# Four heads' scores in one run of matmuls, two PSUM banks for the rest, a filled fourth tile, and ACT as the issuer of attention's stores

## The chip, the cores and the metric

The kernel runs on one core of a Trainium2 chip. The metric is device time in microseconds (us) of one execution; lower is better. The engines are PE (matrix products; PEld is its loading of weights), DVE, ACT and POOL (elementwise work), and SP, which here only issues DMAs. ACT can issue DMAs too; an engine that issues one is occupied while it does so.

## What is computed

Attention over 4 batches, 12 heads, 448 positions and 64 columns per head, in which the heads are mixed twice, then two feed-forward layers over the 1792 rows of 768 columns that attention leaves:

```python
scores = scale * np.matmul(q, k.transpose(0, 1, 3, 2))
scores = np.einsum('bhij,hg->bgij', scores, w_pre)
scores = scores - np.max(scores, axis=-1, keepdims=True)
attn = np.exp(scores)
attn = attn / (np.sum(attn, axis=-1, keepdims=True) + 1e-09)
attn = np.einsum('bhij,hg->bgij', attn, w_post)
x = np.matmul(attn, v)            # then (B, H, S, D) -> (B*S, H*D)
x = (1 / (1 + np.exp(-(x @ w_gate))) * (x @ w_val)) @ w_out
h = np.maximum(x @ w_in, 0.0)
out = h * h @ w_out2
```

## The kernel before

**Attention.** Each batch's 448 rows are cut into four row tiles of 110, 110, 110 and 118 rows, 16 tiles in all; two tiles make a half batch (a chunk, eight in all). `scores(n, p)` makes the scores of two heads (a pair) for tile `n`: four records of PE in the trace (L171), which ACT copies out of PSUM for the one head and DVE for the other (`e`), and which SP stores into `g` so that ten rows of twelve heads lie on 120 partitions. In the tile of 118 rows the last eight rows need a second, small store for each head (L196).

The 180 groups of ten rows are 180 steps of one loop. A step `s` does, in order: `premix(s)`, the first mixing of heads (three matmuls, L219, into `ps_m`); what is pending from the step before (`flush`: the copy `mixed` of postmix's result by DVE, L273, or the copy `valued` of the values by ACT, L305, with its store to `xs`, L306); `maximum(s)` (DVE, L227); `exponent(s-1)` (ACT, L235); `normal(s-2)`, the sum's reciprocal (DVE, L241 and L244) and the weights `wn` that carry it (POOL, L246); and `split(s+2)`, which splits the scores of two steps later into a high part (ACT, `gh`, L209) and a rest (POOL, `gl`, L210). Then a small planner puts in what is owed: `scores` of the next tile, `postmix` (eight records, L261, three steps or more behind) or, once a half batch is mixed, one `values` for each of six steps (16 records, L290). A step's kinds are written here as s (a pair of scores), p (a postmix) and v (values). The planner has a budget for a step and estimated costs:

```python
MW, PW, VW, SW, STEP = 0.62, 0.82, 1.66, 1.04, 2.41
...
            left_over = STEP - MW
            ready = front and front[0][0] <= s
            if ready and due(s):
                next_scores()
```

**Order of DMAs.** SP takes its DMAs in the order of the program: `q` and `k` tiles, `g` stores, `xs` stores, and the six loads `vraw` of a half batch (two heads each, four buffers, so that the fifth load can go when the first values are done). DMAs of SP and ACT use eight semaphores, DMAHW0 to DMAHW7, one after another in the order of the program whichever engine issues them; a DMA is issued only when the one before it on its semaphore has landed. `order` rows show these waits in brackets.

**PSUM.** Eight banks: two for `ps_m`, two for scores (`ps_q`), four (`ps_b`) for postmix and values, which the first tile's scores share.

**The layers after it.** `mlp` is a generator. The attention loop lets it advance in the last 112 steps (`EARLY`), in steps without a postmix, and more freely once all scores are made (`closed`): it loads weights (`w_raw`), splits them (ACT L480, DVE L486 to L509, POOL `w` L520 and `wl` L534) and splits attention's finished columns (`xr`, `xh`, `xl` L596). Its matmuls (L666) stand between the last half batch's values and then fill the rest.

Of the kernel before, what the change touches and what calls it, by code (L numbers as in the profile page):

```python
# [7 lines left out]
F32 = mybir.dt.float32  # L8
# [5 lines left out]
PSUM = bass.MemoryType.PSUM  # L14
DRAM = bass.MemoryType.DRAM

P = 128
JP = 112
GI = 10
# [1 line left out]
LAG = 3  # L21
LA = 5
NA = 9
MW, PW, VW, SW, STEP = 0.62, 0.82, 1.66, 1.04, 2.41
KB = 10
EARLY = 112
EM = 2
# [9 lines left out]

def blocks(b, i0, i1):

    n = (i1 - i0) // GI  # L40
    return [(0, 4), (4, n)] if b == i0 == 0 else [(0, n)]


def row_order(b, i0, i1):

    rows = []
    for g0, g1 in blocks(b, i0, i1):
        rows += [i0 + g * GI + r for r in range(GI) for g in range(g0, g1)]
    return rows + list(range(i0 + len(rows), i1))


def attention(tc, q, k, v, w_pre, w_post, xs, B, H, S, D):
# [10 lines left out]
    nc = tc.nc  # L63
    JT = S // JP
    NP = H // 2
    SCALE = 1.0 / float(D) ** 0.5

    tiles, groups, chunks = [], [], []
# [7 lines left out]
            chunks[-1][4] = len(groups)  # L76
            tiles.append((b, i0, i1 - i0))
    NG = len(groups)
    IM = max(t[2] for t in tiles)
    GT = -(-IM // GI)  # L80
    CM = max(c[2] - c[1] for c in chunks)
    KM = GI * H

    with ExitStack() as ctx, ExitStack() as mid, ExitStack() as left:
        kw = dict(side="right")
# [4 lines left out]
        pa = mid.enter_context(tc.tile_pool(name="a_a", bufs=NA, **kw))  # L90
        pg = mid.enter_context(tc.tile_pool(name="a_g", bufs=2, **kw))
        ph = mid.enter_context(tc.tile_pool(name="a_h", bufs=3, **kw))
        ps_b = ctx.enter_context(tc.tile_pool(name="ps_b", bufs=4, space=PSUM, **kw))
        ps_q = mid.enter_context(tc.tile_pool(name="ps_q", bufs=2, space=PSUM, side="left"))
        ps_m = mid.enter_context(tc.tile_pool(name="ps_m", bufs=2, space=PSUM, side="left"))
        pk = left.enter_context(tc.tile_pool(name="a_k", bufs=KB, side="left"))
        p2 = left.enter_context(tc.tile_pool(name="a_2", bufs=2, side="left"))
# [42 lines left out]
        k_t, q_t = {}, {}  # L140
# [3 lines left out]
            nc.sync.dma_start(out=k_t[b, p], in_=k[b, p])  # L144

        def q_load(n, p0=0, p1=NP):
            b, i0, isz = tiles[n]
            if p0 == 0:
                q_t[n] = p2.tile([P, NP, IM], F32, tag="q", name="q")
            n0, n1 = (b * S + i0) * H * D, (b * S + i0 + isz) * H * D  # L150
            x = q[n0:n1].rearrange("(d p i) -> d p i", d=P, p=NP)
            nc.sync.dma_start(out=q_t[n][:, p0:p1, :isz], in_=x[:, p0:p1])


        g_t, second = {}, []

        def scores(n, p):

            b, i0, isz = tiles[n]
            if p == 0:  # L160
                g_t[n] = pg.tile([KM, GT, S], F32, tag="g", name="g")
            kt = k_t.pop((b, p)) if i0 + isz == S else k_t[b, p]
            ps = [
                ps_b.tile([P, S], F32, tag="b", name="ps_s")
                if n == 0 and p % 2
                else ps_q.tile([P, S], F32, tag="q", name="ps_s")
                for _ in range(2)
            ]
            for o in range(2):
                r = slice(o * D, (o + 1) * D)  # L170
                nc.tensor.matmul(  # L171
                    ps[o][:isz], lhsT=q_t[n][r, p, :isz], rhs=kt[r], start=True, stop=True
                )
            if n == 0 and p >= 3:
                e = [pa.tile([IM, S], F32, tag="a", name="e0") for _ in range(2)]
            else:
                t = p4.tile([IM, 2, S], F32, tag="e", name="e")
                e = [t[:, o] for o in range(2)]
            to = g_t[n].rearrange("(r h) g j -> h r g j", h=H)
            for o in range(2):  # L180
                if o:
                    nc.vector.tensor_copy(e[o][:isz], ps[o][:isz])
                else:
                    nc.scalar.copy(e[o][:isz], ps[o][:isz])
                e0 = 0
                for m, (g0, g1) in enumerate(blocks(b, i0, i0 + isz)):
                    e1 = e0 + (g1 - g0) * GI
                    move = (to[2 * p + o, :, g0:g1], e[o][e0:e1])
                    if m:
                        second.append(move)  # L190
                    else:
                        queue = nc.scalar if n == 0 and o and p in (1, 3, 4, 5) else nc.sync
                        queue.dma_start(out=move[0], in_=move[1])
                    e0 = e1
                if e0 < isz:
                    nc.sync.dma_start(out=to[2 * p + o, : isz - e0, g1], in_=e[o][e0:isz])  # L196


        a_t = {}
# [3 lines left out]
        def split(s):  # L203
            n, r0, rows = groups[s][:3]
            kk = rows * H
            hi = ph.tile([KM, S], F32R, tag="gh", name="gh")
            lo = ph.tile([KM, S], F32R, tag="gl", name="gl")
            x = g_t[n][:kk, r0 // GI]
            nc.scalar.copy(hi[:kk], x)  # L209
            nc.gpsimd.tensor_tensor(out=lo[:kk], in0=x, in1=hi[:kk].bitcast(F32), op=ALU.subtract)  # L210
            parts[s] = (hi[:kk], lo[:kk])
# [39 lines left out]
        ap, pending = {}, []  # L251
# [49 lines left out]
        def valued(c, h, ps):  # L301
            b, i0, i1 = chunks[c][:3]
            w = i1 - i0
            xo = po.tile([P, CM], F32, tag="xo", name="xo")
            nc.scalar.copy(xo[:, :w], ps[:, :w])  # L305
            nc.sync.dma_start(out=xs[b][h * D : (h + 2) * D, i0:i1], in_=xo[:, :w])  # L306


        NT = len(tiles)
# [5 lines left out]
        def load_next(load, order):  # L315
            x = next(order, None)
            if x is not None:
                load(*x)
# [4 lines left out]
            front += [(max(starts[n - 1] - 2, 0), starts[n] - LA, n, p) for p in range(NP)]  # L323
        def due(s):

            return any(z - 1 - i <= s for i, (_, z, _, _) in enumerate(front[:NP]))

        back = []
        for c, ch in enumerate(chunks):
            back += [(postmix, PW, s) for s in range(ch[3], ch[4])]  # L330
            back += [(values, VW, c, h) for h in range(0, H, 2)]
        bpos, closed, posted, behind = 0, False, {}, 0

        def next_scores():
            _, _, n, h = front.pop(0)
            scores(n, h)
            if tiles[n][1] + tiles[n][2] == S:
                load_next(k_load, k_order)
            if h == NP - 1 and n + 1 < NT:
                q_load(n + 1)  # L340

        def flush():
            now, pending[:] = list(pending), []
# [3 lines left out]
        for p in range(0, NP, 2):  # L347
            q_load(0, p, p + 2)
            load_next(k_load, k_order)
            load_next(k_load, k_order)  # L350
        q_load(1)
        masks()
        for p in range(NP):
            scores(0, p)
        mixers()
        for m, (x, y) in enumerate(second):
            (nc.scalar if m % 3 == 1 else nc.sync).dma_start(out=x, in_=y)  # L357
        for s in range(2):
            split(s)
        for s in range(NG + 30):  # L360
            if s < NG:
                premix(s)
            flush()
            if s < NG:
                maximum(s)
            if s in (4, 5, 6, 7):
                load_next(v_load, v_order)
            if 8 <= s < 8 + KB - NP:
                load_next(k_load, k_order)
            if 1 <= s <= NG:  # L370
                exponent(s - 1)
            if 2 <= s < NG + 2:
                normal(s - 2)
            if s + 2 < NG:
                split(s + 2)
            left_over = STEP - MW
            ready = front and front[0][0] <= s
            if ready and due(s):
                next_scores()
                ready, left_over = False, left_over - SW  # L380
            while bpos < len(back) and (left_over > 0.5 or s >= NG):
                f, cost, *x = back[bpos]
                if f is postmix:
                    if x[0] > s - LAG:
                        break
                    posted[groups[x[0]][3]] = s
                elif posted[x[0]] == s:
                    if s < NG:
                        break
                    flush()  # L390
                elif posted[x[0]] == s - 1 and ready:
                    next_scores()
                    ready = False
                if len(pending) > 3:
                    flush()
                f(*x)
                if f is values and (x[1] + 2) % HV == 0:
                    pending.append((load_next, v_load, v_order))
                bpos += 1
                left_over -= cost  # L400
                if f is postmix and x[0] == NG - 1:
                    flush()
                    mid.close()
                if s >= NG:
                    yield 3 if bpos == len(back) or back[bpos][0] is values else 2
            if ready and left_over > 0.4:
                next_scores()
            if not front and not closed:
                left.close()
                closed = True  # L410
            if NG - EARLY <= s < NG:
                behind += 1
                if closed:
                    yield 2
                elif behind >= 3 and s not in posted.values():
                    behind -= 3
                    yield 1
# [406 lines left out]
```

## Time and profile before

| what | value |
|---|---|
| median of 3 executions | 1508.63 us (1508.27 to 1511.84) |
| the profiled execution | 1510.66 us |
| its span in the trace | 1508.9 us |
| mean granted clock of PE | 0.988 of full speed |
| attention, to the last `ps_v` | 0 to 537.3 us |
| matmuls of the layers alone | 537.3 to 1505.4 us |

The span is what the trace covers; the execution's own time is 1.8 us longer. The profiled execution is 2.0 us above the median. Times in the trace are counted from the start of the span.

### The profile page before, as it was taken

Reading aid. Unit: us, or ns where it says so; the run is one execution under the profiler, and the core shown is the slowest. Engines: PE = TensorE matmul, PEld = TensorE weight load, DVE = VectorE, ACT = ScalarE, POOL = GpSimd, SP = SyncE. Lnnn points to the kernel's source line nnn. Section 1 sums busy time; section 2 is a strip of 40 time slices with the busy share of each in tenths; the row PEclk is TensorE's granted clock in tenths of the full one; section 3 lists DMA queues with packets and bytes.
Section 4 is the critical chain, followed back from the end, with each engine's and each line's share of the span. In section 5 each row is a group of like instructions: output and inputs, shape, how many; then the busy total and the mean of one; then the engine's idle time right before and its main releaser. Section 6 shows DMA issues by size and latency. Waiting matters only on the chain.

```text
span 1508.9 us, 22075 instructions
## 1 busy us (share of the span) xinstructions
PE 1468.7 (97%) x8028; PEld 1245.0 (83%) x8028; DVE 809.2 (54%) x1367; ACT 579.6 (38%) x1192; POOL 708.8 (47%) x583
## 2 busy tenths in 40 slices
PE   6989989999998999999999999999999999999999
PEld 3657657667676889999999999999999999999998
DVE  4648657667678577778889999911111001333000
ACT  4545645655655333333234433312222122333111
POOL 3646656766679355555455555532222221222221
PEclk8989999999999999999999999999999999999999
DMA  5453553545534354444444446631211111112221
GB/s 178 140 163 113 150 156 119 168 132 172 167 116 141 113 170 174 156 166 164 158 157 159 163 166 205 217 96 53 63 43 62 53 53 53 53 53 67 75 72 39
DMA packets 87976, 185.47 MB, mean 123 GB/s; under 512 B 18236, under 2 KB 55100, under 8 KB 87868
## 3 DMA queue, kind: packets, MB, share of 16 engines
q1 hardware_dynamic: 87348, 183.28, 38.4%
q8 instruction: 63, 1.03, 0.3%
q10 hardware_dynamic: 520, 0.79, 0.2%
q14 instruction: 45, 0.37, 0.1%
HBM read 107.75 MB, written 37.75 MB: 96 GB/s over the span
## 4 chain that ended last, share of the span: by engine, by line
PE 95%; DMA 2%; POOL 1%; DVE 1%; issue 1%; SPq 0%; ACT 0%; ACTq 0%; POOLq 0%; DVEq 0%
PE ps L666 66%; PE ps_p L261 9%; PE ps_m L219 8%; PE ps_s L171 6%; PE ps_v L290 5%; DMA vraw<-in_v 1%; DMA q<-in_q 0%; POOL gl L210 0%; POOL wn L246 0%; DMA g<-e 0%; DVE ap L273 0%; DMA k<-in_k 0%; ACTq L357 0%; POOL wl L534 0%; DVE nm L227 0%
## 5 line engine op out<-in xcount | busy, mean ns | idle before, releaser
L534 POOL TENSOR_TENSOR wl<-w,wh 128x768 fp32r<-128x768 f32 (+1 forms) x140 | 257.6, 1842 | 550.8 <-ACT wh L526 542.4
L666 PE MATMUL ps<-xh,wh 128*128 128x448 f32 x960 | 351.1, 366 | 0.0
L666 PE MATMUL ps<-xh,wl 128*128 128x448 f32 x960 | 350.7, 365 | 0.0
L666 PE MATMUL ps<-xl,wh 128*128 128x448 f32 x960 | 350.6, 365 | 0.0
L666 PE MATMUL ps<-hh,wl 128*128 128x448 f32 x672 | 246.8, 367 | 0.0
L666 PE MATMUL ps<-hl,wh 128*128 128x448 f32 x672 | 246.8, 367 | 0.0
L666 PE MATMUL ps<-hh,wh 128*128 128x448 f32 x672 | 246.7, 367 | 0.0
L210 POOL TENSOR_TENSOR gl<-g,gh 120x448 fp32r<-120x448 f32 x180 | 208.6, 1160 | 22.2 <-DMA g<-e 18.6
L261 PEld LDWEIGHTS ps_p<-wn,a 120*112 120x112 f32 (+1 forms) x1440 | 165.0, 178 | 43.2 <-issue 20.7
L666 PEld LDWEIGHTS ps<-xh,wh 128*128 128x128 f32 x960 | 180.3, 188 | 15.5 <-issue 1.0
L666 PEld LDWEIGHTS ps<-xh,wl 128*128 128x128 f32 x960 | 180.3, 188 | 14.4 <-POOL wl L534 0.2
L666 PEld LDWEIGHTS ps<-xl,wh 128*128 128x128 f32 x960 | 180.3, 188 | 14.2
L261 PE MATMUL ps_p<-wn,a 120*112 120x120 f32 (+1 forms) x1440 | 177.0, 271 | 6.9 <-POOL wn L246 6.8
L246 POOL TENSOR_SCALAR wn<-wq,sm 120x120 f32<-120x120 f32 x180 | 107.2, 596 | 148.9 <-DVE sm L244 115.4
L520 POOL TENSOR_TENSOR w<-w,w_f 128x768 f32<-128x768 f32 (+1 forms) x70 | 135.4, 1934 | 59.0 <-DVE w_f L509 59.0
L227 DVE TENSOR_REDUCE nm<-ps_m 120x1 f32<-120x448 f32 x180 | 112.0, 622 | 78.9 <-PE ps_m L219 78.6
L684 DVE TENSOR_TENSOR ps<-ps,sg 128x448 f32<-128x448 f32 x48 | 30.4, 632 | 197.2 <-PE ps L666 197.2
L666 PEld LDWEIGHTS ps<-hl,wh 128*128 128x128 f32 x672 | 126.1, 188 | 11.6
L666 PEld LDWEIGHTS ps<-hh,wh 128*128 128x128 f32 x672 | 126.1, 188 | 11.6
L666 PEld LDWEIGHTS ps<-hh,wl 128*128 128x128 f32 x672 | 126.1, 188 | 11.6
L235 ACT ACTIVATE a<-ps_m,nm 120x448 f32<-120x448 f32 x180 | 115.0, 639 | 48.0 <-DVE nm L227 46.6
L273 DVE COPY ap<-ps_p 112x480 f32<-112x480 f32 x180 | 117.0, 653 | 27.2 <-PE ps_p L261 27.2
(45 smaller groups left out, 1693.7 us busy)
## 6 DMA issues: line engine op xcount, KB each, us to landing
g<-e SPq DMA_DIRECT2D x180, 192.5 KB
ws<-w SPq DMA_DIRECT2D x58, 384.0 KB
w<-ws SPq DMA_DIRECT2D x58, 384.0 KB
w_raw<-in_wo SPq DMA_DIRECT2D x18, 768.0 KB
w_raw<-in_wi SPq DMA_DIRECT2D x16, 768.0 KB
vraw<-in_v SPq DMA_DIRECT2D x48, 224.0 KB
w_raw<-in_wg SPq DMA_DIRECT2D x12, 768.0 KB
w_raw<-in_wv SPq DMA_DIRECT2D x12, 768.0 KB
```

The source lines that it names most:

```text
L171: nc.tensor.matmul(ps[o][:isz], lhsT=q_t[n][r, p, :isz], rhs=kt[r], start=True, stop=True)
L210: nc.gpsimd.tensor_tensor(out=lo[:kk], in0=x, in1=hi[:kk].bitcast(F32), op=ALU.subtract)
L219: nc.tensor.matmul(ps[:kk], lhsT=wp[w][:kk, :kk], rhs=x, start=m == 0, stop=m == 2)
L227: nc.vector.tensor_reduce(out=nm[:kk], in_=ps[:kk], op=ALU.max, axis=AX.X, negate=True)
L235: nc.scalar.activation(a[:kk], ps[:kk], AF.Exp, bias=nm[:kk], accum_out=sm[:kk])
L246: nc.gpsimd.tensor_scalar(out=wn[:kk], in0=wq[:kk], scalar1=sm[:kk], scalar2=None, op0=ALU.mult)
L261: nc.tensor.matmul(ps[:JP, jt], lhsT=a[:kk, jt * JP : (jt + 1) * JP], rhs=wn[:kk].rearrange("p g i -> p (g i)"), start=True, stop=True,)
L273: nc.vector.tensor_copy(ap[c][:, :, :, g0 - i0 : g0 - i0 + rows], ps[:JP, :, :, :rows])
L290: nc.tensor.matmul(ps[o * D : (o + 1) * D, :w], lhsT=vraw[c, (h + o) // HV][:, (h + o) % HV, jt, :], rhs=ap[c][:, jt, h + o, :w], start=jt ...
L520: nc.gpsimd.tensor_tensor(out=x[:, s], in0=x[:, s], in1=fs.pop(n)[:, s], op=ALU.add)
L534: nc.gpsimd.tensor_tensor(out=lo[:, s], in0=w32.pop(n)[:, s], in1=h[:, s].bitcast(F32), op=ALU.subtract)
L666: nc.tensor.matmul(ps, lhsT=a, rhs=x, start=first and n == 0, stop=last and n == total - 1)
```

## The change

Four heads' scores are made in one call (`two` pairs, eight PE records in a row), and their banks are four of `ps_q`; `ps_b` keeps two. The planner gets the price of the four heads (1.87), a budget that carries over between steps, and another rule for when scores are due. The fourth tile is filled up to 120 rows by repeating its last row, in `q` as the host lays it out, so that its heads take one `g` store each. The values' stores to `xs` are issued by ACT. `q` of the next tile is loaded when the first pair of a tile is made, and not after its last; the second halves of the first tile's `g` stores stand behind the first two splits.

```diff
-MW, PW, VW, SW, STEP = 0.62, 0.82, 1.66, 1.04, 2.41
+MW, PW, VW, SW, STEP = 0.62, 0.82, 1.66, 1.87, 2.41
...
-    n = (i1 - i0) // GI
+    n = -(-(i1 - i0) // GI)
...
-        ps_b = ctx.enter_context(tc.tile_pool(name="ps_b", bufs=4, space=PSUM, **kw))
-        ps_q = mid.enter_context(tc.tile_pool(name="ps_q", bufs=2, space=PSUM, side="left"))
+        ps_b = ctx.enter_context(tc.tile_pool(name="ps_b", bufs=2, space=PSUM, **kw))
+        ps_q = mid.enter_context(tc.tile_pool(name="ps_q", bufs=4, space=PSUM, side="left"))
...
-                if e0 < isz:
-                    nc.sync.dma_start(out=to[2 * p + o, : isz - e0, g1], in_=e[o][e0:isz])
...
-            nc.sync.dma_start(out=xs[b][h * D : (h + 2) * D, i0:i1], in_=xo[:, :w])
+            nc.scalar.dma_start(out=xs[b][h * D : (h + 2) * D, i0:i1], in_=xo[:, :w])
...
-            return any(z - 1 - i <= s for i, (_, z, _, _) in enumerate(front[:NP]))
+            a, z, _, p = front[0]
+            return s >= a + (p + 1) * (z - a) // NP
...
-            _, _, n, h = front.pop(0)
-            scores(n, h)
-            if tiles[n][1] + tiles[n][2] == S:
-                load_next(k_load, k_order)
-            if h == NP - 1 and n + 1 < NT:
-                q_load(n + 1)
+
+            two = [front.pop(0) for _ in range(2)]
+            for _, _, n, p in two:
+                scores(n, p)
+            for _, _, n, p in two:
+                if tiles[n][1] + tiles[n][2] == S:
+                    load_next(k_load, k_order)
+                if p == 0 and n + 1 < NT:
+                    q_load(n + 1)
...
-        q_load(1)
         masks()
         for p in range(NP):
             scores(0, p)
+        q_load(1)
         mixers()
-        for m, (x, y) in enumerate(second):
-            (nc.scalar if m % 3 == 1 else nc.sync).dma_start(out=x, in_=y)
         for s in range(2):
             split(s)
+        for m, (x, y) in enumerate(second):
+            (nc.scalar if m in (3, 7) else nc.sync).dma_start(out=x, in_=y)
...
-            left_over = STEP - MW
-            ready = front and front[0][0] <= s
+            left_over += STEP - MW
+            ready, made = front and front[0][0] <= s, False
...
-            while bpos < len(back) and (left_over > 0.5 or s >= NG):
+            while bpos < len(back) and (left_over > 0.5 or s >= NG or back[bpos][0] is values and not made):
...
-                if len(pending) > 3:
+                if sum(x[0] in (mixed, valued) for x in pending) > 1:
                     flush()
...
-            if ready and left_over > 0.4:
+            if ready and left_over > 1.2:
                 next_scores()
+                left_over -= SW
+            left_over = min(max(left_over, -0.6), 0.3)
```

PE just behind the first half batch's values, before: a step has one premix, one pair of scores and one postmix (`ps_s ... x2` is a pair).

```order
L261 MATMUL ps_p<-wn,a 112x120 x4
L219 MATMUL ps_m<-gh,wp_125 120x448
L219 MATMUL ps_m<-gh,wp_126 120x448
L219 MATMUL ps_m<-gl,wp_125 120x448
L171 MATMUL ps_s<-k,q 110x448 x2
L261 MATMUL ps_p<-wn,a 112x120 x4
```

The same place of the change: two postmixes in one step, then a step of four heads' scores alone.

```order
L262 MATMUL ps_p<-wn,a 112x120 x8
L220 MATMUL ps_m<-gh,wp_125 120x448
L220 MATMUL ps_m<-gh,wp_126 120x448
L220 MATMUL ps_m<-gl,wp_125 120x448
L174 MATMUL ps_s<-k,q 110x448 x4
L220 MATMUL ps_m<-gh,wp_125 120x448
L220 MATMUL ps_m<-gh,wp_126 120x448
L220 MATMUL ps_m<-gl,wp_125 120x448
L262 MATMUL ps_p<-wn,a 112x120 x8
```

From step 9 to step 178, the steps before are 74 sp or ps, 42 pp, 32 v, 10 sv and 12 p; after they are 63 pp, 39 v, 26 p, 21 ss, 18 pss and 3 ssv (ss: four heads). The first scores that the loop makes, those of the second tile, stand in steps 0 to 5 before, a pair in each, and in steps 0 to 2 after, two pairs in each.

SP in the first half batch's values, before, with its waits: the last `g` stores and loads of the fourth tile and of the next batch, then a store of values and the fifth load of `vraw`.

```order
L193 DMA g<-e 10x11x448 [waits DMAHW1_49,DVE_49]
L196 DMA g<-e 8x448 [waits DMAHW2_49]
L144 DMA k<-in_k 128x448 [waits DMAHW3_49,PE_49]
L152 DMA q<-in_q 128x6x110 [waits DMAHW4_49]
L306 DMA xs_57<-xo 128x220 [waits DMAHW5_49,Activation_49]
L280 DMA vraw<-in_v 112x512 [waits DMAHW6_49,PE_49]
```

SP at the same place of the change.

```order
L196 DMA g<-e 10x12x448 [waits DMAHW0_49,DVE_49]
L196 DMA g<-e 10x12x448 [waits DMAHW1_49,Activation_49]
L196 DMA g<-e 10x12x448 [waits DMAHW2_49,DVE_49]
L148 DMA k<-in_k 128x448 [waits DMAHW3_49,PE_49]
L148 DMA k<-in_k 128x448 [waits DMAHW4_49,PE_49]
L281 DMA vraw<-in_v 112x512 [waits DMAHW5_49,PE_49]
```

And ACT there, from the third to the fourth values of this half batch: its two stores are the DMAs that stand before those two loads of `k` on DMAHW3 and DMAHW4.

```order
L306 COPY xo<-ps_v 128x220 [waits PE_49]
L307 DMA xs_57<-xo 128x220 [waits DMAHW3_49,Activation_49]
L236 ACTIVATE a,sm<-ps_m,nm 120x448 [waits DVE_49]
L210 CAST gh<-g 120x448 [waits Pool_49]
L306 COPY xo<-ps_v 128x220 [waits PE_49]
L307 DMA xs_57<-xo 128x220 [waits DMAHW4_49,Activation_49]
```

The `xs` stores have left SP, and the fifth load of `vraw` now stands behind two `k` loads whose semaphores ACT's third and fourth store held last.

POOL at the end of attention's steps, before (the last five `gl`).

```order
L210 TENSOR_TENSOR gl<-g,gh 120x448
L534 TENSOR_TENSOR wl<-w_5414,wh 128x768
L246 TENSOR_SCALAR wn<-wq,sm 120x120
L210 TENSOR_TENSOR gl<-g,gh 120x448
L246 TENSOR_SCALAR wn<-wq,sm 120x120
L210 TENSOR_TENSOR gl<-g,gh 120x448
L596 TENSOR_TENSOR xl<-xr,xh 128x448
L246 TENSOR_SCALAR wn<-wq,sm 120x120
L210 TENSOR_TENSOR gl<-g,gh 96x448
L246 TENSOR_SCALAR wn<-wq,sm 120x120 x3
```

The same place of the change.

```order
L211 TENSOR_TENSOR gl<-g,gh 120x448
L247 TENSOR_SCALAR wn<-wq,sm 120x120
L211 TENSOR_TENSOR gl<-g,gh 120x448
L247 TENSOR_SCALAR wn<-wq,sm 120x120
L211 TENSOR_TENSOR gl<-g,gh 120x448
L247 TENSOR_SCALAR wn<-wq,sm 120x120
L211 TENSOR_TENSOR gl<-g,gh 96x448
L247 TENSOR_SCALAR wn<-wq,sm 120x120 x3
```

The layers' `wl` and `xl` have left this stretch; they now stand eight to ten `gl` earlier, in the steps of the last half batch but one's values.

## Rows read from the trace of the kernel before

**Rows 1.** Chain that ended last: start, length (us), what it was in.

```profile
38.17 7.05 DMA q<-in_q
...
96.24 4.52 DMA vraw<-in_v
...
451.35 2.81 DMA vraw<-in_v
...
537.30 968.07 PE ps L666 x4752
```

**Rows 2.** Windows: length, busy us of PE, PEld, DVE, ACT, POOL, clock, DMA, GB/s.

```profile
206.00:229.00 23.00, 18.63 (x125) 11.43 (x124) 6.29 (x21) 9.39 (x27) 10.11 (x12) 0.85 0.75 224
...
459.00:497.00 38.00, 31.41 (x222) 26.45 (x221) 30.46 (x73) 20.12 (x50) 34.02 (x36) 0.96 0.35 105
```

**Rows 3.** Timeline of PE, steps with a pair of scores each, 79 to 83.

```profile
79.76 0.67 PE L219 MATMUL ps_m<-gh,wp 120*120 120x448 f32 x2
...
82.32 0.67 PE L219 MATMUL ps_m<-gh,wp 120*120 120x448 f32 x2
```

**Rows 4.** Timeline of all engines, the steps after a tile's last pair, 60 to 64.

```profile
60.59 0.67 PE L219 MATMUL ps_m<-gh,wp 120*120 120x448 f32 x2
...
60.73 0.62 DVE L182 COPY e<-ps_s 110x448 f32<-110x448 f32 x1 [0.57 <-PE ps_s L171]
...
62.04 0.65 PE L219 MATMUL ps_m<-gh,wp 120*120 120x448 f32 x2
...
63.45 1.07 PE L261 MATMUL ps_p<-wn,a 120*112 120x120 f32 x8 [0.56 <-POOL wn L246]
...
64.28 0.65 PE L219 MATMUL ps_m<-gh,wp 120*120 120x448 f32 x2
```

**Rows 5.** Chain that ended last, in the values of the third half batch.

```profile
205.33 0.96 PE ps_s L171 x4
206.30 1.64 PE ps_v L290 x16
207.94 0.80 PE ps_m L219 x3
```

**Rows 6.** Timeline of PEld, the first tile's pairs, 11 to 12.

```profile
11.14 0.17 PEld L171 LDWEIGHTS ps_s<-k,q 64*110 64x110 f32 x1 [0.20 <-issue]
11.52 0.17 PEld L171 LDWEIGHTS ps_s<-k,q 64*110 64x110 f32 x1 [0.20 <-issue]
```

**Rows 7.** Timeline of PE, the first premix of step 9 and that of step 11.

```profile
40.82 0.65 PE L219 MATMUL ps_m<-gh,wp 120*120 120x448 f32 x2
...
50.35 0.66 PE L219 MATMUL ps_m<-gh,wp 120*120 120x448 f32 x2
```

**Rows 8.** Timeline of SP's queue, stores of the fourth tile, 72 to 95.

```profile
73.60 0.70 SPq L196 DMA_DIRECT2D g<-e  x1
...
94.41 0.39 SPq L144 DMA_DIRECT2D k<-in_k  x1
```

**Rows 9.** Waits, of the engines and of SP's queue: us in total, times, longest.

```profile
PE ps_v L290 <- DMA vraw<-in_v: 13.9, 4, 7.0
...
SPq L280 <- DMA q<-in_q: 0.8, 1, 0.8
```

**Rows 10.** Timeline of PE and ACT around the first wait for `vraw`.

```profile
93.03 0.67 PE L219 MATMUL ps_m<-gh,wp 120*120 120x448 f32 x2
...
93.14 0.34 ACT L305 COPY xo<-ps_v 128x220 f32<-128x220 f32 x1 [1.01 <-PE ps_v L290]
...
107.88 0.66 PE L219 MATMUL ps_m<-gh,wp 120*120 120x448 f32 x2
```

**Rows 11.** Timeline of DVE and PE in steps with two postmixes, 133 to 136.

```profile
133.92 0.66 DVE L273 COPY ap<-ps_p 112x480 f32<-112x480 f32 x1
...
135.16 1.80 PE L261 MATMUL ps_p<-wn,a 120*112 120x120 f32 x16
```

**Rows 12.** Groups of DVE to 500 us: count, busy us, mean ns, idle before.

```profile
L489 DVE SCALAR_TENSOR_TENSOR w<-w_f,w_t 128x768 uint32<-128x768 uint32 x3 | 3.8, 1261 | 0.1
```

More of the change, by code (lines that the diff above doesn't have):

```diff
@@ L47, in row_order @@
     for g0, g1 in blocks(b, i0, i1):
-        rows += [i0 + g * GI + r for r in range(GI) for g in range(g0, g1)]
-    return rows + list(range(i0 + len(rows), i1))
+        rows += [min(i0 + g * GI + r, i1 - 1) for r in range(GI) for g in range(g0, g1)]
+    return rows
 def attention(tc, q, k, v, w_pre, w_post, xs, B, H, S, D):
@@ L78, in attention @@
     NG = len(groups)
-    IM = max(t[2] for t in tiles)
-    GT = -(-IM // GI)
+    full = [-(-t[2] // GI) * GI for t in tiles]
+    IM = max(full)
+    GT = IM // GI
     CM = max(c[2] - c[1] for c in chunks)
@@ L146, in q_load @@
         def q_load(n, p0=0, p1=NP):
-            b, i0, isz = tiles[n]
             if p0 == 0:
                 q_t[n] = p2.tile([P, NP, IM], F32, tag="q", name="q")
-            n0, n1 = (b * S + i0) * H * D, (b * S + i0 + isz) * H * D
+            n0, isz = sum(full[:n]) * H * D, full[n]
+            n1 = n0 + isz * H * D
             x = q[n0:n1].rearrange("(d p i) -> d p i", d=P, p=NP)
@@ L157, in scores @@
         def scores(n, p):
-            b, i0, isz = tiles[n]
+            b, i0, rows = tiles[n]
+            isz = full[n]
             if p == 0:
                 g_t[n] = pg.tile([KM, GT, S], F32, tag="g", name="g")
-            kt = k_t.pop((b, p)) if i0 + isz == S else k_t[b, p]
+            kt = k_t.pop((b, p)) if i0 + rows == S else k_t[b, p]
             ps = [
-                ps_b.tile([P, S], F32, tag="b", name="ps_s")
-                if n == 0 and p % 2
-                else ps_q.tile([P, S], F32, tag="q", name="ps_s")
+                ps_q.tile([P, S], F32, tag="q", name="ps_s")
                 for _ in range(2)
@@ L185, in scores @@
                 e0 = 0
-                for m, (g0, g1) in enumerate(blocks(b, i0, i0 + isz)):
+                for m, (g0, g1) in enumerate(blocks(b, i0, i0 + rows)):
                     e1 = e0 + (g1 - g0) * GI
@@ L331, in attention @@
             back += [(values, VW, c, h) for h in range(0, H, 2)]
-        bpos, closed, posted, behind = 0, False, {}, 0
+        bpos, closed, posted, behind, left_over = 0, False, {}, 0, 0
         def next_scores():
-            _, _, n, h = front.pop(0)
-            scores(n, h)
-            if tiles[n][1] + tiles[n][2] == S:
-                load_next(k_load, k_order)
-            if h == NP - 1 and n + 1 < NT:
-                q_load(n + 1)
+            two = [front.pop(0) for _ in range(2)]
[6 more added lines that the diff above has]
+                    q_load(n + 1)
         def flush():
@@ L392, in attention @@
                     next_scores()
-                    ready = False
-                if len(pending) > 3:
+                    ready, left_over = False, left_over - SW
+                if sum(x[0] in (mixed, valued) for x in pending) > 1:
                     flush()
                 f(*x)
+                made = made or f is values
                 if f is values and (x[1] + 2) % HV == 0:
```

## The prediction

> **What bounds the kernel now.** I read the chain that ended last first. Its last piece is 968 us of the layers' matmuls, which follow one another from 537.3 us with no wait [rows 1]. Nothing of the change reaches into that stretch, so whatever attention gains or loses before 537 us moves the end by the same amount. In the chain before it PE's own work is nearly everything, with a few pieces of DMA in between: the load of `q` at 38 us and the fifth load of `vraw` in every second half batch. So I read attention by the length of a step of PE, premix to premix, for each kind of step, then the list of waits, then the windows in which PE idles.
>
> Three lengths carry the argument. A step with a postmix and a pair of scores takes 2.56 us (79.76 to 82.32) [rows 3]. A step with a postmix alone takes 1.45 us when nothing is late (60.59 to 62.04) [rows 4]. A values step takes 0.80 + 1.64 = 2.44 us [rows 5]. The three ways in which PE waits are `wn` (0.56 us once in rows 4, and in the last steps), `q` (once), and `vraw` (13.9 us in four waits) [rows 4, 9].
>
> **The change, part by part.**
>
> *Scores in one run.* A pair costs 2.56 - 1.45 = 1.11 us in a postmix step and 0.96 us before values [rows 5]. It has two rounds of records, so a lone round is taken as half of 0.96, 0.48. In the first tile, where pairs follow one another, rounds begin 0.38 us apart (11.14, 11.52) [rows 6]. A second pair right behind the first therefore adds 0.76 us: four heads cost 1.87 us, or 1.72 before values. From step 9 on there are 84 pairs. Before: 74 x 1.11 + 10 x 0.96 = 91.7. After: 39 x 1.87 + 3 x 1.72 = 78.1. Gain **+13.6**; with 0.48 in place of 0.38 for the two rounds it is 13.6 - 42 x 0.2 = 5.2 (a rival, below).
>
> *A rule against it.* In rows 6 the weights of a next round are loaded 0.38 us after those of the round before, less than the 0.48 of a lone round, so part of the load is hidden there. The Trainium skill, "TensorE: Matmul & The Clock Gate", section "The mechanism", says that a weight load overlaps a running matmul only where its row group differs, and the rounds of two pairs use the same rows: by that rule every round would take its full 0.48 and the gain would be the 5.2. The trace disagrees in these two rows, and the sum goes by them.
>
> *The stall behind a double.* Behind a pair DVE copies `e` (60.73) before that step's `mixed` and maximum, so the reciprocal and `wn` two postmixes on come late: the step from 62.04 to 64.28 takes 2.24 us and not 1.45 [rows 4]. Before, this appears once after a run of pairs, since in sp steps 2.56 us leave DVE room. After, DVE has two copies in a row, and doubles alternate with lone postmixes. By the order ten postmixes stand two steps behind a double with a double of their own (steps 11, 13, 22, 24, 45, 47, 90, 92, 135, 137). 10 x 0.8 = **-8**. Bounds: 0, if the longer step of the double covers it; -14, if DVE's second copy (0.62) comes on top of the 0.8 each time.
>
> *The load of `q`.* The second `q` after the start is issued only at 38.17 and lands 7.05 later [rows 1]. Steps 9 and 10 take 9.53 us (40.82 to 50.35) [rows 7] where two steps with a pair take 5.12. After the change it is issued with the first doubles, some 20 us earlier. Gain **+4.4**. In front of step 9 the start gains by the `q` load of the second tile, which leaves SP's way, and loses by `g` stores that now stand in one run behind the second halves of the first tile; I take **0**, from -2 to +2 (about a postmix step of 1.45 lost or won, estimated).
>
> *The wait for `vraw`.* Two causes must be told apart. SP stores the fourth tile's heads with two DMAs each, the small one 0.70 us [rows 8], and is behind until 94.41; the fifth `vraw` is issued at 96.24, lands 4.52 later, and PE stands still for 7.0 us [rows 1, 9]. The change takes these small stores (48 in all) and the `xs` stores off SP. But in the new order that load stands behind two `k` loads on the semaphores of ACT's third and fourth `xs` store, and a DMA waits for the one before it on its semaphore (the trace of before has SP wait for a `q` load in this way) [rows 9]. So count from the premix of the fifth values' step. ACT's copy starts 0.11 later and takes 0.34 [rows 10], the issue about 0.4 like a `k` load's 0.39 [rows 8], landing I estimate at 1.2 us, between that issue and the 2.81 us in which a load of twice the size lands at the least [rows 1]: 2.0. Then a `k` issue, 0.4, and the load, 2.81 to 4.52, taken as 3.4: 5.8. Values are due at 0.8. PE waits 5.0 in place of 7.0. In the third half batch a load of `xr` stands between as well, another 0.4: 5.4 in place of 4.37 (23.00 less 18.63) [rows 2]. The last two waits, 2.5 together, I leave. Each wait also costs some 2 to 3 us of slower PE after it (steps 29 and 30 take 14.85 where 4.88 would do: 7.0 idle, 3.0 slow) [rows 10], where the window shows a mean clock of 0.85 [rows 2]; that stays too. Net **+1**. Bounds: -4.5 (landing takes 2.81 and the load 4.52 twice) to +21 (all gone, a rival).
>
> *ACT's stores.* ACT idles 1.01 us in a values step [rows 10] and an issue takes 0.4, so **0** here. If that cover is gone every store costs its 0.4.
>
> *The layers' preparation.* In the order POOL's `wl` and `xl` leave the last steps, where POOL is busy 34.0 of 38.0 us and PE idles 6.6 [rows 2], and go to values steps, where 2.44 us leave POOL room. I take **+5** (2 to 6.6). On the other side pieces for DVE of up to 1.26 us [rows 12] now fall into four steps in which DVE also copies two heads (83, 103, 125, 148), where they push `mixed` past its margin: 4 x 0.8 = **-3.2** (0 to -5).
>
> *Two banks.* With two postmixes a step, a `mixed` ends at 134.58 and the postmix that would need its bank starts at 135.16: 0.58 us of margin [rows 11], so **0** in the 63 such steps. If that cover were gone, each 0.1 us late costs 6.3. Three values in a row at the very end now have two banks: **-1** (0 to -2). Two rows more in the fourth tile: 2/118 of 0.96 for 24 pairs would be 0.4 us, taken as 0.
>
> Sum: 13.6 - 8 + 4.4 + 0 + 1 + 0 + 5 - 3.2 + 0 - 1 = **11.8 us** less. The profiled execution took 1510.66, so 1498.9; it was 2.03 above the median, so **1496.8**. A measurement of this kernel tells about 0.3%, 4.5 us, from no change.
>
> **Rivals.**
>
> *The `vraw` waits vanish.* If SP's backlog were the whole cause, the load would be issued 12 x 0.75 = 9 us earlier, at 87, and land before 93.8. For it: 94.41 and 96.24 in SP's queue. Against it: the order's semaphores. It gives the 13.9 us and some 7 of slower PE, less the 1 counted: 20 more, 1477; with only the first two gone about 1481.
>
> *Rounds stay 0.48 apart.* The lone pairs show it, the first tile doesn't. It takes 8.4 away: 1505.2.
>
> *Slower: ACT and SP wait for one another.* ACT's stores, too, wait for the DMA before them on their semaphore, which is SP's, and ACT's queue then holds up `exponent` and `gh`, for which PE waits a step or two later. The place is the 42 values of the first seven half batches. Cover is 1.01 - 0.4 = 0.6 us a step. The point from which it decides: a mean wait of 0.6 + 11.8/42 = 0.9 us per store. At 1.1 us it costs 21: 1518. For it: SP's DMAs in the fourth tile wait for landings all the time. Against it: by the order the DMAs in question (`k`, `q` and `g`) were issued a step or more before.
>
> **How the numbers follow.** The sum 0.50, with a range of its own from 1490 to 1504; the waits vanish 0.18; rounds stay 0.10; ACT and SP 0.12; and 0.10 that several of the smaller terms end near no change. Faster by over 0.3% (below 1504.1): 0.49 + 0.18 + 0.04 + 0.02 = 0.73. Within: 0.01 + 0.06 + 0.06 = 0.13. Slower: 0.12 and 0.02 of the last, 0.14. The range from 1481 to 1508 leaves out the ACT case and a third of the vanished waits, about 0.18.
>
> **What would show it.** Right: rounds 0.38 apart in four-head runs; a step of four heads and a postmix near 3.3 us, followed by waits of PE for `wn` of about 0.8, ten of them; no wait for `q` after 38 us; `vraw` still waited for, some 13 us in four waits, released by a load issued right after ACT's fourth store landed; PE's idle time in the last 20 steps near 1 us. Wrong: rounds 0.48 apart, no `vraw` waits, ACT's exponent late in values steps, or postmix waiting for DVE's `mixed` in steps of two.

## The result and the profile after

The change makes the kernel slower: 1527.63 us (median of four executions, 1526.76 to 1529.59) against 1509.18 us (the kernel before, four executions), a ratio of 1.0124 with a 95% interval of 1.0107 to 1.0142. Forecast were 1496.8 us and a range from 1481 to 1508. The profiled execution has a span of 1526.4 us.

Between the two profiled executions the spans differ by 17.5 us (1526.4 less 1508.9), and the chain that ended last says where they sit. Its columns are those of [rows 1].

```profile
102.14 3.09 DMA xs<-xo
105.72 2.90 DMA vraw<-in_v
108.75 3.20 PE ps_v L291 x16
...
118.83 1.69 PE ps_s L174 x8
...
223.91 2.02 DMA xs<-xo
226.90 4.44 DMA vraw<-in_v
...
347.19 6.23 DMA xs<-xo
353.48 2.75 DMA vraw<-in_v
...
466.20 3.05 DMA xs<-xo
...
554.84 968.03 PE ps L674 x4752
```

The last piece is as long as in [rows 1] (968.07) and begins 17.5 us later: all of the loss is in attention. Ahead of the fifth `vraw` there is now a store of the values on the chain, in three of the four half batches in which the kernel before waited. In the fourth (466.20) it is not `vraw` that the chain goes on to but POOL, which waits before it makes `xl` for the layers. The list of waits of the changed kernel (engine and line, releaser: us, times, longest) puts sizes to it; the second part is that of SP's queue.

```profile
ACT e L187 <- DMA g<-e: 22.2, 8, 4.8
DVE e L185 <- DMA g<-e: 21.9, 9, 4.6
...
PE ps_v L291 <- DMA vraw<-in_v: 19.6, 3, 7.2
...
POOL xl L604 <- DMA xs<-xo: 6.2, 1, 6.2
...
PE ps_m L220 <- POOL gl L211: 3.8, 1, 3.8
```

```profile
SPq L281 <- DMA xs<-xo: 19.7, 7, 6.4
SPq L196 <- DMA xs<-xo: 18.9, 7, 3.5
...
SPq L587 <- DMA xs<-xo: 7.4, 2, 3.8
```

PE's wait for `vraw` has risen from 13.9 us [rows 9] to 19.6. SP stands in front of `vraw` loads, `g` stores and `xr` loads until a store issued by ACT has landed, 46 us in these three rows. And there is a wait that hardly existed before (ACT 2.2 us, now 22.2): ACT and DVE can't copy scores out because the buffer `e` is still being stored.

By premixes (the first one of a step, before and after) the 17.6 us up to step 178 divide like this. A plus is time lost.

| steps | before us | after us | difference |
|---|---|---|---|
| to premix 20 | 69.30 | 75.43 | +6.1 |
| 20 to 25 | 13.02 | 14.66 | +1.6 |
| 25 to 31 (values of half batch 1) | 25.56 | 25.62 | +0.1 |
| 31 to 70 | 96.59 | 94.77 | -1.8 |
| 70 to 76 (half batch 3) | 23.38 | 28.03 | +4.7 |
| 76 to 115 | 96.62 | 95.18 | -1.4 |
| 115 to 121 (half batch 5) | 20.51 | 28.77 | +8.3 |
| 121 to 160 | 96.58 | 96.42 | -0.2 |
| 160 to 166 (half batch 7) | 16.82 | 22.06 | +5.2 |
| 166 to 178 | 31.10 | 26.12 | -5.0 |

The start and the values of three half batches lose 24 us. Elsewhere the change does nearly what was predicted of it.

### The profile page after: what moved, and what is told of

It is laid out like the page before. It is cut to its first block, busy times and chain, and to the rows that moved or that the text cites. A ratio compares the mean times of both kernels' runs of the same rounds, so it can differ in the third digit from the quotient of the medians.

```text
span 1526.4 us, 22029 instructions
## 1 busy us (share of the span) xinstructions
PE 1463.9 (96%) x8028; PEld 1252.3 (82%) x8028; DVE 807.6 (53%) x1367; ACT 585.0 (38%) x1192; POOL 707.5 (46%) x583
## 4 chain that ended last, share of the span: by engine, by line
PE 86%; POOL 5%; DMA 4%; issue 3%; ACT 1%; DVE 1%; SPq 0%; POOLq 0%; ACTq 0%; DVEq 0%
PE ps L674 65%; PE ps_p L262 7%; PE ps_m L220 5%; PE ps_v L291 4%; PE ps_s L174 4%; POOL gl L211 3%; POOL wn L247 2%; DMA g<-e 2%; DMA xs<-xo 1%; DMA vraw<-in_v 1%; ACT a L236 0%; DVE e L185 0%; DMA k<-in_k 0%; ACT e L187 0%; DVE nm L228 0%
## 5 line engine op out<-in xcount | busy, mean ns | idle before, releaser
L262 PE MATMUL ps_p<-wn,a 120*112 120x120 f32 (+1 forms) x1440 | 172.4, 271 | 11.2 <-POOL wn L247 8.1
L220 PE MATMUL ps_m<-gh,wp 120*120 120x448 f32 x360 | 121.6, 419 | 13.4 <-ACT a L236 8.0
```

The lines of the kernel that those rows point to most:

```text
L220: nc.tensor.matmul(ps[:kk], lhsT=wp[w][:kk, :kk], rhs=x, start=m == 0, stop=m == 2)
L262: nc.tensor.matmul(ps[:JP, jt], lhsT=a[:kk, jt * JP : (jt + 1) * JP], rhs=wn[:kk].rearrange("p g i -> p (g i)"), start=True, stop=True,)
```

## The experiments

Two theories stand against one another. **A**: the three buffers `e`, each of a pair, hold less than two calls of four heads, and the copies wait for `g` stores. **B**: the stores that ACT issues hold up SP through the semaphores that both use in turn. A third question is what the kernel before waited for at `vraw`.

**A fourth buffer.**

```diff
-        p4 = left.enter_context(tc.tile_pool(name="a_4", bufs=3, side="left"))
+        p4 = left.enter_context(tc.tile_pool(name="a_4", bufs=4, side="left"))
```

> The changed kernel (1527.6 us) with four buffers for the score copies e in place of three. Theory A (three buffers hold fewer than two calls of four heads, so the copies of ACT and DVE wait for g stores to land, 22 us each in the trace, and PE behind them at steps 2 to 4, 14 to 16, 71, 116 and 117): a fourth buffer takes away half or more of these waits, 1517 to 1521. Theory B (the stores issued by ACT, and the eight semaphores that they share with SP, are the whole loss): 1525 to 1529.

Measured: 1540.21 us, ratio to before 1.0196 (1.0174 to 1.0219), slower by 12.6 us than the change itself. Neither theory had this. The list of waits:

```profile
PE ps_v L291 <- DMA vraw<-in_v: 40.8, 6, 12.0
...
DVE e L185 <- DMA g<-e: 2.7, 2, 2.4
ACT e L187 <- DMA g<-e: 2.5, 1, 2.5
```

```profile
SPq L196 <- DMA xs<-xo: 39.3, 14, 4.6
```

The copies' waits are nearly gone, and premix 20 comes at 68.25 in place of 75.43, so A is right about the start. But the waits for `vraw` double, and appear in the half batches 2, 4 and 6 too. In front of `g` stores SP now waits 39.3 us for ACT's stores (the row of its queue above), twice the 18.9 of the change.

**Stores on SP again.**

```diff
-            nc.scalar.dma_start(out=xs[b][h * D : (h + 2) * D, i0:i1], in_=xo[:, :w])
+            nc.sync.dma_start(out=xs[b][h * D : (h + 2) * D, i0:i1], in_=xo[:, :w])
```

> The changed kernel with the stores to xs issued by SP again. Theory B: the waits for the fifth vraw in the half batches 3, 5 and 7 (11.2, 10.2 and 7.6 us steps) go back to the lengths of the kernel before or below, since that load then stands behind one store and not behind four: 1510 to 1516. Theory A: the waits for e remain and little changes, 1524 to 1529.

Measured: 1511.39 us, ratio 1.0009 (0.9995 to 1.0023): one word takes back 16.2 us.

```profile
ACT e L187 <- DMA g<-e: 23.4, 8, 4.6
DVE e L185 <- DMA g<-e: 21.8, 9, 4.4
...
PE ps_v L291 <- DMA vraw<-in_v: 8.5, 2, 4.6
```

B holds in its place, and A's waits are untouched by it: there are two losses, not one. By premixes, the values of half batches 1, 3 and 5 take 18.7, 23.1 and 23.7 us in place of 25.6, 28.0 and 28.8, together 16.9 less; those of half batch 7 take 22.4, no less than in the change (22.1). That ACT spends time on issuing is not the cause: PE waits as long for ACT's `a` with the stores on SP (7.7 us) as in the change (8.0). What is left in half batch 7 is this, in the list of the run with the stores on SP:

```profile
POOL xl L604 <- DMA ws<-w: 5.9, 1, 5.9
...
PE ps_m L220 <- POOL gl L211: 3.6, 1, 3.6
```

**The filled tile alone, on the kernel before.** Of the change only the rows that fill the fourth tile, and with them 48 fewer `g` stores.

```diff
-                if e0 < isz:
-                    nc.sync.dma_start(out=to[2 * p + o, : isz - e0, g1], in_=e[o][e0:isz])
```

> The kernel before with the fourth tile filled up to 120 rows and nothing else of the change: 48 small stores leave SP. If SP's backlog is what the kernel before waits for at vraw (the rival of the prediction), the load is issued about 9 us earlier in the first half batch and the waits of 13.9 us and the slow PE after them go: 1489 to 1493. If the semaphores are what it waits for, 1503 to 1508.

Measured: 1493.54 us, ratio 0.9888 (0.9864 to 0.9913), the fastest of all runs here, with one other (1493.78) beside it. Of its list of waits and its chain:

```profile
PE ps_v L290 <- DMA vraw<-in_v: 2.5, 2, 1.7
```

```profile
517.07 968.02 PE ps L666 x4752
```

13.9 us of waiting become 2.5, and the layers begin at 517.1. The kernel before waited for SP's backlog of small stores; in front of its `vraw` loads SP waited only 0.8 us for a DMA to land [rows 9].

**The old order of the start**, in the changed kernel.

```diff
+        q_load(1)
         masks()
         for p in range(NP):
             scores(0, p)
-        q_load(1)
         mixers()
+        for m, (x, y) in enumerate(second):
+            (nc.scalar if m % 3 == 1 else nc.sync).dma_start(out=x, in_=y)
         for s in range(2):
             split(s)
-        for m, (x, y) in enumerate(second):
-            (nc.scalar if m in (3, 7) else nc.sync).dma_start(out=x, in_=y)
```

> The changed kernel with the start of the kernel before: the second tile's q loaded first, the second halves of the first tile's g stores before the two splits and dealt to SP and ACT as before. If the new order of the start costs what it lost there (premix of step 9 at 46.3 in place of 40.8), 1521 to 1524. If the e buffers are the cause of that loss, whatever the order, 1526 to 1529.

Measured: 1526.49 us (1.0107, 1.0084 to 1.0130), no different from the change by what the intervals tell. Premix 20 comes at 75.23 (75.43). The order of the start isn't what costs.

**ACT's stores on top of the filled tile**, single pairs as before: the edit of the stores, the other way round.

> The kernel before with the filled fourth tile (1493.5 us) and, on top, the stores to xs issued by ACT; single pairs of scores as before. Theory B (in the order of the eight semaphores SP's q or vraw load then stands behind ACT's third or fourth store of a half batch, whatever the scores' calls look like): the waits for vraw come back, some 4 to 8 us each in three half batches, 1504 to 1514. Rival (ACT's stores cost only together with the calls of four heads): 1491 to 1496.

Measured: 1512.35 us (1.0024, 1.0010 to 1.0038), 18.8 us slower than the filled tile alone. The list of waits, then that of SP's queue:

```profile
PE ps_v L290 <- DMA vraw<-in_v: 18.2, 7, 8.1
```

```profile
SPq L280 <- DMA xs<-xo: 25.5, 12, 4.3
```

B holds without the calls of four heads: ACT's stores alone undo what the filled tile gives. The values of half batches 1 and 3 are 8.8 and 5.0 us longer than with the filled tile alone; half batch 7 is not (16.6 against 16.5).

**Stores on SP and a fourth buffer**, in the changed kernel: the first two edits together.

> The changed kernel with the stores on SP (alone 1511.4) and four buffers e (alone 1540.2, where the waits for e went from 22 to 3 us and those for vraw rose from 20 to 41). If the fourth buffer's gain was hidden there by the semaphores alone, both add here: 1500 to 1505. If buffers give nothing to the end in any case: 1509 to 1513.

Measured: 1500.02 us (0.9953, 0.9932 to 0.9973), 11.4 us less than with the stores on SP alone. Premix 20 comes at 67.73 in place of 78.11, which is 10.4 of it. So the fourth buffer gives what A says once ACT's stores are away. The rest of its list:

```profile
PE ps_v L291 <- DMA vraw<-in_v: 12.8, 3, 6.2
...
DVE e L185 <- DMA g<-e: 4.2, 2, 2.3
ACT e L187 <- DMA g<-e: 4.0, 2, 2.4
```

With calls of four heads `vraw` is still late (12.8 us, against 2.5 with single pairs), and this version stays 6.5 us behind the filled tile alone.

**DVE's last copy of a call behind the next maximum**, in the version with stores on SP and a fourth buffer.

```diff
             for o in range(2):
+                if o and wait:
+                    later.append((to[2 * p + 1, :, : full[n] // GI], e[1][:isz], ps[1][:isz]))
+                    continue
...
                 normal(s - 2)
+            rest()
```

> The kernel of the run beside it (stores on SP, four buffers e), and DVE's copy of a call's last head stands behind the next step's maximum and reciprocal. If that copy is what makes wn late behind four heads, 4.1 us steps become 3.4 to 3.5 in ten places and the first values step behind them is short again: 7 to 10 us less than the run beside it. If POOL or PE sets those steps: no change.

Measured: 1504.05 us (0.9970, 0.9957 to 0.9983), 4.0 us more where 7 to 10 less were forecast; the intervals of the two overlap. In its own place the edit does what the reason said, though less. First premixes of steps 44, 45, 46 and 48 in the version without it and then with it:

```profile
129.25 0.65 PE L220 MATMUL ps_m<-gh,wp 96*96 96x448 f32 x2
...
130.68 0.65 PE L220 MATMUL ps_m<-gh,wp 120*120 120x448 f32 x2
...
134.79 0.66 PE L220 MATMUL ps_m<-gh,wp 120*120 120x448 f32 x2
...
140.34 0.67 PE L220 MATMUL ps_m<-gh,wp 120*120 120x448 f32 x2
```

```profile
136.38 0.66 PE L231 MATMUL ps_m<-gh,wp 96*96 96x448 f32 x2
...
137.83 0.64 PE L231 MATMUL ps_m<-gh,wp 120*120 120x448 f32 x2
...
141.59 0.66 PE L231 MATMUL ps_m<-gh,wp 120*120 120x448 f32 x2
...
146.80 0.66 PE L231 MATMUL ps_m<-gh,wp 120*120 120x448 f32 x2
```

The step of a double is 3.76 us in place of 4.11, and the stretch 10.42 in place of 11.09. But premix 20 comes 1.4 us later, and the first half batch's values lose 6.1 us, with a wait for `vraw` of 4.8 us in place of 0.6. The head copied later is stored later, which may be why; no run shows it.

**The next `q` at the first pair**, on the filled tile, and then **the same with a fourth buffer**.

```diff
-            if h == NP - 1 and n + 1 < NT:
+            if h == 0 and n + 1 < NT:
                 q_load(n + 1)
```

> The kernel before with the filled fourth tile (1493.5 us) and the next tile's q loaded when the first pair of a tile is made. If the wait for q at steps 9 and 10 is worth the 4.4 us of the prediction: 1487 to 1490. If the load only shifts the wait to g stores behind it: 1492 to 1495.

> The kernel before with the filled fourth tile, the next tile's q at the first pair (1497.4 with three buffers, where the copies e waited 13 us for g stores in place of 1) and a fourth buffer e. If those waits for landed g stores are what took the gain of the early q: 1486 to 1490. If the fourth buffer again moves waits to vraw: 1493 to 1500.

Measured: 1497.38 us (0.9925, 0.9906 to 0.9945) and 1493.78 us (0.9906, 0.9883 to 0.9929), against 1493.54. The first is 3.8 us above it where a gain of 4.4 was priced, and outside both of its forecasts (its interval overlaps that of the filled tile). Steps 9 and 10 win 3.0 us, but the two steps from 14 lose 3.3 again: ACT's waits for `g` stores went from 0.7 to 13.1 us. With the fourth buffer these are gone, and no gain is left; at step 74 of its trace `vraw` is waited for again (the shift against the filled tile grows by 5.2 us there). The traced execution took 1498.91 us, 5.1 above the median. The early `q` brought nothing measurable to the whole here.

**`vraw` loaded by ACT**, in the changed kernel.

```diff
-            nc.sync.dma_start(out=t, in_=v[chunks[c][0], hv])
+            (nc.scalar if c or hv > 3 else nc.sync).dma_start(out=t, in_=v[chunks[c][0], hv])
```

> The changed kernel (1527.6 us) with the loads of vraw issued by ACT, right behind the store of the values that freed their buffer, and so no longer behind SP's loads of k, xr and w_raw. If the place of the load behind SP's waits for ACT's stores is what makes vraw late: the waits of 19.6 us and the slow PE behind them go, 1503 to 1511. If ACT's queue, with two issues in a values step and waits on SP's semaphores, then holds up exponent and gh: 1520 to 1530.

Measured: 1531.88 us (1.0156, 1.0140 to 1.0172), just above the second forecast. No row of PE waiting for `vraw` is left in the list of waits; in its place stands the first row below, which was 8.0 us in the change. The second is from SP's queue.

```profile
PE ps_m L220 <- ACT a L236: 28.8, 16, 3.9
```

```profile
SPq L196 <- DMA vraw<-in_v: 38.4, 10, 12.4
```

The wait moves with the DMA: now SP's stores wait for loads that ACT issued, and ACT's own work is late.

**Stores issued by POOL**, in the changed kernel.

```diff
-            nc.scalar.dma_start(out=xs[b][h * D : (h + 2) * D, i0:i1], in_=xo[:, :w])
+            nc.gpsimd.dma_start(out=xs[b][h * D : (h + 2) * D, i0:i1], in_=xo[:, :w])
```

> The changed kernel with the stores to xs issued by POOL, whose DMAs have semaphores of their own. If the shared semaphores are the loss (and not that the stores left SP's queue): near the run with the stores on SP, 1508 to 1514, plus what POOL's issue costs it in values steps. If the order on SP alone makes the loss: 1524 to 1530.

Measured: 1523.78 us (1.0092, 1.0073 to 1.0111), between the two forecasts. Its list of waits has the reason:

```profile
POOL xs L307 <- ACT xo L306: 42.6, 13, 9.7
...
PE ps_v L291 <- DMA vraw<-in_v: 7.5, 2, 5.2
...
PE ps L674 <- POOL wl L542: 4.1, 2, 2.7
```

In SP's queue no wait for an `xs` store is left, PE's wait for `vraw` is as short as with the stores on SP (8.5), and premix 121 comes at 348.10 (348.17 with the stores on SP). So up to 348 us it is the shared semaphores and not the order of the rest of SP's queue. After that POOL, which takes its stores in order, stands before them until ACT has copied the last values (the first row; 25.8 us of it, in 6 waits, lie between 480 and 600 us), and `wl` for the layers is late (4.1 us of waiting in the last row, which the run with the stores on SP doesn't have). The trace ends 10.3 us later than that one's, 2.8 of them by step 178.

## Why the prediction was wrong

**The score term (13.6) was right in kind.** A run of four heads takes 1.69 us (the chain above) where the prediction had 1.72 before values, and the weights of its rounds are loaded 0.38 us apart:

```profile
151.02 0.18 PEld L174 LDWEIGHTS ps_s<-k,q 64*110 64x110 f32 x2 [0.20 <-issue]
151.40 0.18 PEld L174 LDWEIGHTS ps_s<-k,q 64*110 64x110 f32 x2 [0.20 <-issue]
```

So the rival of 0.48 fell. By the measurement the Trainium skill's rule on row groups ("TensorE: Matmul & The Clock Gate", "The mechanism"), as the prediction used it, doesn't hold for these rounds.

**The stall behind a double (-8) was right, and a little small.** PE in the changed kernel, steps 43 to 46:

```profile
143.41 0.64 PE L220 MATMUL ps_m<-gh,wp 120*120 120x448 f32 x2
...
146.70 0.65 PE L220 MATMUL ps_m<-gh,wp 96*96 96x448 f32 x2
...
148.13 0.65 PE L220 MATMUL ps_m<-gh,wp 120*120 120x448 f32 x2
...
149.55 1.07 PE L262 MATMUL ps_p<-wn,a 120*112 120x120 f32 x8 [0.57 <-POOL wn L247]
...
152.25 0.67 PE L220 MATMUL ps_m<-gh,wp 120*120 120x448 f32 x2
```

The first double's step takes 3.29 us, the next one's 4.12, with the wait for `wn` that [rows 4] had shown: 0.82 against 0.8. All ten places have it (4.08 to 4.11), and the late copy above took 0.35 of it away, so DVE's second copy is a part of the cause. Not counted was the values step behind the last double of a stretch, 3.02 us where the others take 2.49, in the half batches 2, 4 and 6. The pieces for DVE (-3.2) cost less, some 1.8 if all of this is theirs: the pp steps 85, 127, 151 and 152 take 2.59, 3.38, 2.43 and 2.35 us in place of 2.25. Together with the scores, the parts of the table between the values (steps 20 to 25, 31 to 70, 76 to 115, 121 to 160) sum to -1.8 us, where the terms had some -3.

**The layers' preparation (+5) was right where it left, and wrong where it went.** Steps 166 to 178 win 5.0 us. But the values of half batch 7, where `wl` and `xl` now stand, lose 5.2, and 3.8 of it is PE's wait for a `gl` that stands behind `xl` on POOL. The words "values steps, where 2.44 us leave POOL room" counted POOL's work and not that `xl` would wait 6.2 us there until DMAs have landed. ACT's stores aren't the cause: with the stores on SP and with POOL as issuer this stretch takes 22.4 and 22.0 us too. `xl` waits for several semaphores at once, and the profile names another DMA in different versions, so which one it is stays open. The two banks cost next to nothing: most pp steps take 2.25 us as before. The last us, for three values in a row, did not come (4.77 us for them before and after).

**The first step that failed: "In front of step 9 ... I take 0, from -2 to +2".** It counted SP's issues and not how long a buffer `e` is held. The wait for `q` went, as priced (steps 9 and 10 take 5.00 in place of 9.53 us), but premix 20 is 6.1 us later and not 3.9 earlier (4.4 for `q`, 1.1 for the first doubles, less two stalls of 0.8): 10 us. The experiments show the cause of most of it: a fourth buffer brings premix 20 forward by 7.2 us with ACT's stores and by 10.4 without, and the old order of the start does nothing. At best premix 20 comes at 67.73, still 2.3 us behind the forecast; that rest stays open.

**The second: the `vraw` term (+1), in its sizes.** The values of half batches 1, 3 and 5 lose some 13 us in the table, and moving the stores back to SP takes 16.9 from these three. The mechanism was named (loads behind ACT's stores on a shared semaphore), its sizes were wrong. The landing of a store was estimated at 1.2 us; on the chain it is 3.09, 2.02 and 6.23, and PE waits 6.2, 7.2 and 6.2 us where 5.0, 5.4 and the 2.4 of the kernel before had been counted. SP's `g` stores and loads of `k` and `xr` wait for ACT's stores as well (above), so that the third wait, which "I leave", grew most; the fourth, left too, is gone. And the copies of `e` wait in the values steps 71, 116 and 117.

**The rivals.** "The `vraw` waits vanish" had the right cause: the filled tile alone gives 17 us by its ratio (0.0112 x 1509), 16.0 by the medians (1509.6 less 1493.5). I argued against it with the semaphores, which became a cost only because the stores moved to ACT. So one part of the change wins 16 to 17 us, and another, 16.2 or 18.8 by the two experiments, takes them back. "ACT and SP wait for one another" came nearest in time (1518) and had the direction wrong: it is SP that waits for ACT's stores. It came near by luck, then, and not by its mechanism.

What stays open besides: why, with ACT's stores out of the way, bunches of four heads' stores still leave `vraw` late (12.8 us against 2.5). More buffers for `vraw` were not tried.

## What to carry to other kernels

A DMA that goes to another engine's queue takes its semaphore along: where queues share completion semaphores in turn, the queue that it left waits for it to land, wherever its next turn falls, so look at what stands eight DMAs on. When work is bunched, count how many buffers the bunch holds at once and until their stores have landed, not only the banks and the engines. And price the parts of a change apart: here one edit alone was worth 16 us and could be had without the rest.

## What was not expected of the hardware

Three stores of 110 KB on the chain took 2.0 to 6.2 us from issue to landing, where the estimate from a load's 2.81 us had been 1.2. After each of PE's three waits for `vraw` (6.2 to 7.2 us) the first values take 3.20 us in place of 1.64. In the stretch from 219 to 239 us, in which PE stands still for 7.2 us, the granted clock (the row's 0.74, of full speed) is lower on the mean than the 0.982 of the whole:

```profile
219.00:239.00 20.00, 12.82 (x78) 7.77 (x77) 3.40 (x12) 6.28 (x17) 7.89 (x9) 0.74 0.60 171
```

Steps 74 and 75 take 15.1 us where 4.9 would do. So a wait of 7.2 us there costs some 10 in the end, like the first one of the kernel before (7.0 idle, 3.0 slow).
